# Gated state-space convolution and dense layer: the transforms' second stage and its inverse on sums and differences of mirrored samples

## The chip, the cores and the metric

The kernel runs on one core of one Trainium2 chip. The metric is device time in microseconds for one execution, from launch to the last write. Engines are named as in the profile: PE is TensorE's matmuls, PEld its weight loads, DVE is VectorE, ACT ScalarE, POOL GpSimd and SP SyncE, which here only issues transfers (SPq).

## What is computed

```python
def _A_ref(u, A_re, A_im, B_re, B_im, C_re, C_im, log_dt, Dskip):   # u: 1 x 2048 x 512
    dt = exp(log_dt)[:, None]
    P = exp((dt * A)[:, :, None] * arange(L))                       # 512 x 128 x 2048
    K = einsum("dn,dnl,dn->dl", C, P, dt * B).real                  # the convolution's taps
    y = irfft(rfft(u padded to 2L) * rfft(K padded to 2L))[:L]      # along the 2048 positions
    return y + u * Dskip

def _B_ref(x, w1, b1, w2, b2):                                      # 512 -> 1792 -> 512
    return gelu(x @ w1 + b1) @ w2 + b2

x = A_u
g = sigmoid((x * gate_w).sum(-1, keepdims=True))
return g * _A_ref(x, ...) + (1 - g) * _B_ref(x, ...)
```

All of it is in float32, with 2048 positions and 512 channels.

## The kernel before

The program has two parts. `front` holds the dense layer, the making of the taps, and the first stage of both transforms. `conv` holds the second stages, the product of the spectra, the inverse and the output.

**The transform.** The 2048 positions are split as 64 p + q, with p up to 32 and q up to 64. A first stage transforms over p: its result is, for each of 32 frequencies k0, the real and imaginary parts of 64 values of q, 128 rows by 512 channels. It goes to memory (`tu_d` for the signal, `tk_d` for the taps) and comes back one k0 at a time as a 256 KB tile (`attic` and `loft` for the signal, `tk` for the taps). The second stage multiplies such a tile with a matrix over q, once for the real part and once for the imaginary part of 64 outputs k1.

**`front`** does not run in the order in which it is written. Four generators (`dense`, `taps`, `signal`, `early`) add tasks with an engine, a length and a due time to `Plan`, and `Plan.run` sorts them into one order for each engine. Each engine then runs its instructions strictly in that order. Lengths and due times are constants of the file (`K_0`, `D_S1` and so on). `dense` is the 512-1792-512 layer, in float32 split into a high and a low part, so that each product is three matmuls (L869 to L871 for the first matrix, L917 to L919 for the second). `taps` makes K in 16 contractions of 32 channels (`contract`, L653): 64 matmuls each, of 128 by 32 weights on 64 columns, into the PSUM tile `pk`. ACT copies `pk` to `s1` (L670), and after every second contraction `first_stage` (L378) makes eight matmuls of 32 by 64 weights, two into each of four PSUM banks. ACT copies these into `sk` (L678). After four contractions, eight transfers take `sk` to `tk_d` (L693), in runs of 256 bytes. `signal` loads two tiles of x, runs the same `first_stage` on them, eight times in all, and stores to `tu_d` (L399). POOL's queue carries a memset for each contraction (L605), the loads of `xh` and `xlo` (L772) and the accumulating output transfers (L949).

**`conv`** is written out by hand as 16 steps of two frequencies each. In a step, DVE makes the product of the spectra, six operations on 128x512 (L1106 to L1111, `product`). PE makes the second stage of the next step's signal and of the taps two steps ahead (L1084, `pair`), and this step's inverse (L1123, `inverse`). ACT copies the taps' results out of PSUM (L1092) and the inverse's (L1129, tile `sa`). SP stores each `sa` to `t4_d` (L1131), fetches later tiles of taps and signal (L1059, L1179) and, from step 6 on, the dense layer's output (L1148). Every second step, `matrices` makes on ACT the second half of the weights out of a loaded table `cc` (L1068 to L1071). After every four steps the stored results come back with positions as columns and frequencies as rows in `t3` (L1138), on POOL's queue, the last time on ACT's. After the last step PE does the rest of the dense layer (`rest`, L1159 to L1161) and four matmuls on old data (`warm`, L1197). The last stage (L1208) then multiplies 64 rows of `t3` at a time with 64 by 32 weights. Its results are scaled by the gate and added to the dense output on DVE (L1219), or on ACT and POOL (L1216, L1217), and stored.

## Time and profile before

| what | value |
|---|---|
| time, median of 3 runs | 552.75 us (551.3 to 552.95) |
| span of the profiled execution | 549.7 us |
| PE busy | 528.3 us (96%) |
| DVE busy | 427.2 us (78%) |
| ACT busy | 371.6 us (68%) |
| POOL busy | 41.2 us (7%) |
| transfers | 108.35 MB, 82469 packets, 39446 of them under 512 bytes |
| chain that ended last, by engine | PE 65%, ACT 13%, DMA 7%, issue 6% |

The profile is of one execution. A busy PE says only that a matmul was in its pipeline, since matmuls overlap. The chain that ended last is found by going back from the last instruction to what released it, so it names the work that set the end. A row of instructions gives line, engine, operation, output and inputs, shape, count, busy time and mean nanoseconds of one; a float32 matmul shows as two records, one for each of its passes. In a table of windows each engine has its busy microseconds and its count, then follow the granted clock of PE, the mean busy share of the 16 DMA engines, and the bytes moved per second.

### The profile page before, as it was taken

How to read it: one execution, taken by the hardware profiler on the slowest of the kernel's cores; microseconds unless marked ns; L12 is line 12 of the kernel's file. 1: busy time of each engine (PE TensorE's matmuls, PEld its weight loads, DVE VectorE, ACT ScalarE, POOL GpSimd, SP SyncE). 2: the span in 40 equal slices, each digit the busy share in tenths (PEclk: the TensorE clock that was granted, in tenths of full speed). 3: DMA queues.
4: the chain of work that ended last, by engine and by line, in shares of the span. 5: the costliest groups of instructions: out<-in, count | busy, mean ns of one | idle time of the engine just before them, and what ended most of it. 6: DMA issues, size and time to landing. Idle time of an engine off the chain costs nothing.

```text
span 549.7 us, 12354 instructions
## 1 busy us (share of the span) xinstructions
PE 528.3 (96%) x4882; PEld 394.7 (72%) x4882; DVE 427.2 (78%) x806; ACT 371.6 (68%) x630; POOL 41.2 (7%) x79
## 2 busy tenths in 40 slices
PE   7879999999999999999999999999999999999993
PEld 6547887988798879787988889889889633333450
DVE  6798999999999949879999899999411566666523
ACT  4979847799856599977668987397263654555312
POOL 2000000000000000000101010101011001010104
PEclk9868999999999999999999999999999999999997
DMA  8989573153592442483976136624528979999968
GB/s 252 342 282 312 188 254 113 48 185 111 128 277 97 154 114 80 150 300 63 221 209 183 39 72 149 126 79 109 162 39 184 305 253 302 377 395 377 315 230 305
DMA packets 82469, 108.35 MB, mean 197 GB/s; under 512 B 39446, under 2 KB 42522, under 8 KB 81900
## 3 DMA queue, kind: packets, MB, share of 16 engines
q1 hardware_dynamic: 77020, 86.56, 49.0%
q0 software_dynamic: 5056, 18.65, 13.2%
q10 hardware_dynamic: 336, 2.36, 1.2%
q8 instruction: 38, 0.62, 0.5%
q14 instruction: 19, 0.16, 0.1%
HBM read 61.93 MB, written 45.62 MB: 196 GB/s over the span
## 4 chain that ended last, share of the span: by engine, by line
PE 65%; ACT 13%; DMA 7%; issue 6%; DVE 3%; SPq 2%; POOL 1%; POOLq 0%; ACTq 0%; DVEq 0%
PE pk L653 9%; PE acc L917 7%; PE ph L869 7%; PE ph L871 7%; PE ph L870 7%; PE acc L919 6%; PE acc L918 6%; PE p2u L1084 5%; PE p2k L1084 5%; PE pa L1123 4%; ACT sk L678 2%; PE ph L378 2%; ACT L886 2%; DMA tu_d<-attic 2%; ACT ph L886 1%
## 5 line engine op out<-in xcount | busy, mean ns | idle before, releaser
L869 PE MATMUL ph<-xh,wh 128*128 128x256 f32 x448 | 129.7, 289 | 3.7 <-ACT attic L396 1.5
L871 PE MATMUL ph<-xh,wl 128*128 128x256 f32 x448 | 128.6, 287 | 0.5 <-DVE wl L752 0.4
L870 PE MATMUL ph<-xlo,wh 128*128 128x256 f32 x448 | 128.3, 286 | 0.0
L869 PEld LDWEIGHTS ph<-xh,wh 128*128 128x128 f32 x448 | 86.9, 194 | 13.3 <-issue 4.8
L917 PE MATMUL acc<-wh,hh 128*128 128x512 f32 x210 | 87.1, 415 | 2.6 <-ACT hh L889 2.5
L870 PEld LDWEIGHTS ph<-xlo,wh 128*128 128x128 f32 x448 | 87.0, 194 | 2.0
L871 PEld LDWEIGHTS ph<-xh,wl 128*128 128x128 f32 x448 | 86.9, 194 | 1.1 <-DVE wl L752 1.1
L919 PE MATMUL acc<-wh,hl 128*128 128x512 f32 x210 | 83.0, 395 | 0.0
L918 PE MATMUL acc<-wl,hh 128*128 128x512 f32 x210 | 82.9, 395 | 0.0
L886 ACT ACTIVATE ph<-ph,b1t 128x256 f32<-128x256 f32 x112 | 50.4, 450 | 40.3 <-PE ph L871 38.4
L899 DVE TENSOR_TENSOR hl<-ph,hh 128x512 fp32r<-128x512 f32 (+1 forms) x62 | 38.4, 620 | 37.7 <-ACT hh L889 37.6
L653 PE MATMUL pk<-y,xc 128*32 128x64 f32 x2048 | 61.4, 290 | 0.0
L653 PEld LDWEIGHTS pk<-y,xc 128*32 128x32 f32 x2048 | 57.2, 136 | 3.7 <-issue 1.4
L917 PEld LDWEIGHTS acc<-wh,hh 128*128 128x128 f32 x210 | 39.7, 189 | 21.9 <-issue 11.2
L919 PEld LDWEIGHTS acc<-wh,hl 128*128 128x128 f32 x210 | 39.7, 189 | 10.5 <-DVE hl L899 1.7
L615 DVE TENSOR_TENSOR y<-y,ea 128x64 f32<-128x64 f32 (+4 forms) x80 | 45.4, 567 | 0.2
L918 PEld LDWEIGHTS acc<-wl,hh 128*128 128x128 f32 x210 | 39.8, 189 | 6.0
L889 ACT CAST hh<-ph 128x512 fp32r<-128x512 f32 (+1 forms) x62 | 33.0, 532 | 9.1 <-PE acc L918 7.3
L460 DVE TENSOR_TENSOR loft<-xc,zz 128x256 f32<-128x256 f32 (+2 forms) x48 | 37.3, 777 | 1.7 <-ACT xc L586 1.2
L461 DVE TENSOR_TENSOR loft<-xc,zz 128x256 f32<-128x256 f32 (+2 forms) x48 | 37.2, 775 | 0.0
L628 DVE TENSOR_TENSOR y<-y,loft 128x2048 f32<-128x2048 f32 x16 | 36.6, 2286 | 0.0
L1092 ACT COPY k<-p2k 128x512 f32<-128x512 f32 x32 | 18.7, 586 | 22.0 <-issue 12.2
(172 smaller groups left out, 926.6 us busy)
## 6 DMA issues: line engine op xcount, KB each, us to landing
tu_d<-attic SPq DMA_DIRECT2D x64, 128.0 KB, 3.1
tk_d<-sk SPq DMA_DIRECT2D x32, 256.0 KB, 4.5
tk<-tk_d SPq DMA_DIRECT2D x32, 256.0 KB, 5.6
t_d<-sa SPq DMA_DIRECT2D x32, 256.0 KB, 5.1
t<-t_d POOLq DMA_DIRECT2D x12, 512.0 KB, 6.6
attic<-tu_d SPq DMA_DIRECT2D x22, 256.0 KB, 4.5
attic<-in_xt_dram SPq DMA_DIRECT2D x16, 256.0 KB, 3.9
xh_d<-xh SPq DMA_DIRECT2D x8, 512.0 KB, 3.8
```

Of the source, the lines that this page charges most:

```text
L460: vec(2 * m, lambda: vv.tensor_mul(t, a, br), due, [ka, *kb], [kt])
L615: nc.vector.tensor_mul(both(n, 64 - 3 * n, n), both(0, 64 - n, n), an)
L653: nc.tensor.matmul(pks[q][32 * j : 32 * j + 32, gg], x[:, r, :, ch], y[:, r, :, ch], start=(r == 0), stop=(r == 1), skip_group_check=True,)
L869: nc.tensor.matmul(p, h, xh[xk][:, d], start=(d == 0), stop=False)
L870: nc.tensor.matmul(p, h, xlo[xk][:, d], start=False, stop=False)
L871: nc.tensor.matmul(p, lo, xh[xk][:, d], start=False, stop=(d == 3))
L886: nc.scalar.activation(phs[q][:, n], phs[q][:, n], AF.Gelu_apprx_tanh, bias=b1t[:, f : f + 1])
L899: nc.vector.tensor_sub(lo, phs[q][:, 0:nf], hi.bitcast(F32))
L917: nc.tensor.matmul(a, h, wh[1][w], start=start, stop=False)
L918: nc.tensor.matmul(a, h, wl[1][w], start=False, stop=False)
L919: nc.tensor.matmul(a, l, wh[1][w], start=False, stop=(j == 3))
L1084: nc.tensor.matmul(out[64 * i : 64 * i + 64], w, x, start=True, stop=True)
```

## The change

The tiles that the second stage reads hold sums and differences of mirrored positions in place of real and imaginary parts. The real part of the spectrum then depends on the first 64 rows alone, through cosines, and the imaginary part on the last 64 rows alone, through sines. So each 128 by 64 product becomes a 64 by 64 one, and the same holds for the inverse: 64 by 64 weights into one half of the output's rows, without a second accumulating matmul. The table of weights has four pieces of 384 KB in place of eight of 256 KB, and `matrices` is gone. The recombination of sums and differences moves into the last stage, whose weights grow from 64 by 32 to 128 by 64.

The sums and differences are made on POOL: for the signal from pairs of loaded tiles, 128x512 each, and for the taps from `s1`, 128x256 each, between the contraction and the first stage. For the latter the contraction writes its 64 columns 32 bytes apart in PSUM (`[P, 64, 8]`). The row order of input and output and the order of the channels change with it; the constants that set the planner's due times do not. The diff, without the numbering of rows on the host, the renamed tables of constants and moved declarations:

```diff
+    c1 = np.stack([np.stack([er, ei], 2), np.stack([ei, -er], 2)], 1).reshape(32, 128)
+    c1 = np.tile(c1, (4, 1))
...
+    f2 = np.zeros((32, 2, 2, 32, 64))
+    g2 = np.zeros((32, 64, 32, 2))
     for n, k in enumerate(ko):
-        er, ei = om(4 * (q[:, None] * k + 32 * np.outer(q, k1)) + q[:, None])
-        f2[n, 0], f2[n, 1] = er, -ei
-        er, ei = om(4 * (qn[None] * k + 32 * np.outer(k1, qn)) + qn[None])
-        g2[n, :, :, 0], g2[n, :, :, 1] = er, -ei
-    f2 = f2.reshape(8, 4, P, 64).transpose(0, 2, 1, 3).reshape(8, P, 256)
-    g2 = g2.reshape(8, 2, P, P).transpose(0, 2, 1, 3).reshape(8, P, 256)
+        a = 2.0 * np.pi * (k + 32 * k1 + 0.25) / L
+        f2[n, :, 0] = np.cos(np.outer(m + 0.5, a))
+        f2[n, :, 1] = np.sin(np.outer(m + 0.5, a))
+        g2[n, :, :, 0] = np.cos(np.outer(a, m))
+        g2[n, :, :, 1] = np.sin(np.outer(a, m))
+        g2[n, :, 0, 1] = 1 - 2 * (k1 % 2)
...
-        pks = tiles(N_PK, [P, 8, 64], "pk", space=psum)
+        pks = tiles(N_PK, [P, 64, 8], "pk", space=psum)
         pus = tiles(N_PU, [P, D], "pu", space=psum)
 
-        sk = pool.tile([P, 64, 2, 4, 8], F32, name="sk")
+        sk = pool.tile([P, 32, 4, 4, 8], F32, name="sk")
-        s1 = tiles(2, [P, D], "s1")
+        s1 = tiles(2, [P, 2, 256], "s1")
+        sd = tiles(2, [P, 2, 256], "sd")
...
-                        nc.tensor.matmul(bank[64 * m : 64 * m + 64], c1t[rs], x[rs], start=True, stop=True)
-
-            mm(1.2, products, due + D_S1, [*(key for _, key in xs), "c1"], [key for _, key in banks], 0.5)
+                        nc.tensor.matmul(bank[64 * m : 64 * m + 64], c1t[rs, m], x[rs], start=True, stop=True)
+
+            keys = [k for _, key in xs for k in (key if isinstance(key, list) else [key])]
...
-        rows = tu_d.rearrange("k (c t) d -> (k c) t d", c=2)
+        rows = tu_d.rearrange("k (c e t) d -> (k c) e t d", c=2, e=2)
...
-                xs = [(ux[m], ("ux", m)) for m in range(2)]
                 for m in range(2):
-                    move(256, lambda m=m, s=s: nc.sync.dma_start(ux[m], xl[2 * s + m]), t - 10, [], [("ux", m)])
+                    move(256, lambda m=m, s=s: nc.sync.dma_start(ux[m], xl[s + 8 * m]), t - 10, [], [("ux", m)])
+                k = take("ld", N_LD)
+                pl.add(
+                    "POOL", 1.27, lambda k=k: nc.gpsimd.tensor_add(ld[k], ux[0], ux[1]), t - 9,
+                    [("ux", 0), ("ux", 1)], [("ld", k)],
+                )
+                pl.add("POOL", 1.27, lambda: nc.gpsimd.tensor_sub(ux[1], ux[0], ux[1]), t - 9, [("ux", 0)], [("ux", 1)])
...
-                first_stage(xs, t, evac)
+                first_stage([(ld[k], ("ld", k)), (ux[1], ("ux", 1))], t, evac)
...
-                                pks[q][32 * j : 32 * j + 32, gg],
+                                pks[q][32 * j : 32 * j + 32, :, gg],
...
-            xs, key = s1[c % 2], ("s1", c % 2)
-            act(512, lambda: nc.scalar.copy(xs, pks[q].rearrange("p g s -> p (g s)")), t + D_S1, [("pk", q)], [key])
-            pair.append((xs, key))
-            if c % 2 == 0:
+            e = c % 2
+            xs, key = s1[e], ("s1", e)
+            act(512, lambda: nc.scalar.copy(xs, pks[q].rearrange("p (e s) g -> p e (s g)", e=2)), t + D_S1, [("pk", q)], [key])
+            pl.add(
+                "POOL", 0.7, lambda: nc.gpsimd.tensor_add(sd[0][:, e], xs[:, 0], xs[:, 1]), t + D_S1,
+                [key], [("sd", 0, e)],
+            )
+            pl.add(
+                "POOL", 0.7, lambda: nc.gpsimd.tensor_sub(sd[1][:, e], xs[:, 0], xs[:, 1]), t + D_S1,
+                [key], [("sd", 1, e)],
+            )
+            if e == 0:
...
-                        sk[:, :, c // 2, r].rearrange("p s g -> p g s"),
-                        pp.rearrange("p (g s) -> p g s", g=8),
+                        sk[:, :, cs, r].rearrange("p s e g -> p e s g"),
+                        pp.rearrange("p (e s g) -> p e s g", e=2, g=8),
...
-            first_stage([pair.pop(0), pair.pop(0)], t, evac)
+            first_stage(
+                [(sd[i].rearrange("p a b -> p (a b)"), [("sd", i, 0), ("sd", i, 1)]) for i in range(2)], t, evac
+            )
...
-                n, ss = h % 2, slice(h // 2 * 16, h // 2 * 16 + 16)
-                d = u * UW + n * 64
+                n, ss = h % 2, slice(h // 2 * 8, h // 2 * 8 + 8)
+                d = u * UW
...
-                        tk_d[:, :, d : d + 64].rearrange("k (c s) g -> (k c) s g", c=2)[:, ss],
+                        tk_d[:, :, d : d + UW].rearrange("k (c e s) g -> (k c) e s g", c=2, e=2)[:, n, ss],
...
-            if n % 4 == 0:
-                m = n // 4
-                cc = pool.tile([P, 2, 256], F32, tag="cc", name=f"cc{m}", bufs=4)
-                nc.sync.dma_start(cc, c2[m].rearrange("p (a b) -> p a b", a=2))
-                c4s[m] = cc
+            if n % 8 == 0:
+                m = n // 8
+                cc = pool.tile([P, 768], F32, tag="cc", name=f"cc{m}", bufs=4)
+                nc.sync.dma_start(cc, c2[m])
+                mats[m] = cc[:, 0:512].rearrange("p (n k) -> p n k", n=8), cc[:, 512:768].rearrange("p (n k) -> p n k", n=4)
...
-        def matrices(m):
-
-            cc = c4s[m]
-            f = cc[:, 0].rearrange("p (n k) -> p n k", n=4)
-            f1 = pool.tile([P, 4, 64], F32, tag="f1", name=f"f1{m}", bufs=2)
-            g = cc[:, 1].rearrange("p (s q c) -> p s q c", s=2, c=2)
-            g1 = pool.tile([P, 2, 64, 2], F32, tag="g1", name=f"g1{m}", bufs=2)
-            nc.scalar.mul(f1[0:64], f[64:128], -1.0)
-            nc.scalar.copy(f1[64:128], f[0:64])
-            nc.scalar.mul(g1[:, :, :, 0], g[:, :, :, 1], -1.0)
-            nc.scalar.copy(g1[:, :, :, 1], g[:, :, :, 0])
-            mats[m] = (f, f1), [z.rearrange("p s q c -> p s (q c)") for z in (g, g1)]
...
-        def pair(s, r, c, out):
+        def pair(s, r, outs):
 
             for i in range(2):
                 n = 2 * s + i
-                w = mats[n // 4][0][c][:, n % 4]
                 x = t2s[n] if r else us[n % N_US]
-                nc.tensor.matmul(out[64 * i : 64 * i + 64], w, x, start=True, stop=True)
+                w = mats[n // 8][0][:, n % 8]
+                for c in range(2):
+                    h = slice(64 * c, 64 * c + 64)
+                    nc.tensor.matmul(outs[c][64 * i : 64 * i + 64], w[h], x[h], start=True, stop=True)
...
+            pks = [ps.tile([P, D], F32, tag="pk", name=f"p2k{s}{c}", bufs=2) for c in range(2)]
+            pair(s, 1, pks)
...
-                pas[2 * s + i] = ps.tile([P, D], F32, tag="pa", name=f"pa{s}{i}", bufs=2)
-            for c in range(2):
-                w = mats[s // 2][1][c][:, s % 2]
-                for i in range(2):
-                    r = slice(64 * i, 64 * i + 64)
-                    nc.tensor.matmul(pas[2 * s + i], w[r], v[c][r], start=(c == 0), stop=(c == 1))
+                n = 2 * s + i
+                pas[n] = ps.tile([P, D], F32, tag="pa", name=f"pa{s}{i}", bufs=2)
+                r = slice(64 * i, 64 * i + 64)
+                w = mats[n // 8][1][r, s % 4]
+                for c in range(2):
+                    nc.tensor.matmul(pas[n][64 * c : 64 * c + 64], w, v[c][r], start=True, stop=True)
...
-                nc.sync.dma_start(t4_d[g, :, :, k].rearrange("i c q d -> q (i c) d"), sa)
-                if k < GROUP - 1:
-                    continue
-                rows = t4_d[g].rearrange("i c k q d -> (i c k) q d")
-
-                for h in range(0, 32, 8):
-                    on = nc.gpsimd if n < 31 else nc.scalar
...
+                for c in range(2):
+                    nc.sync.dma_start(t4_d[g, c, :, k].rearrange("e q d -> q e d"), sa[64 * c : 64 * c + 64])
+            if k < GROUP - 1:
+                return
+            rows = t4_d[g].rearrange("c e k q d -> (c e k) q d")
+
+            for h in range(0, 32, 8):
+                on = nc.gpsimd if s < 15 else nc.scalar
...
-            for b in range(4):
-                for i in range(2):
-                    r = slice(64 * i, 64 * i + 64)
+            for i in range(2):
+                for b in range(2):
+                    j = 4 * m + 2 * i + b
                     nc.tensor.matmul(
-                        pbs[i][32 * b : 32 * b + 32], g1t[r], t3[r, 4 * m + b], start=True, stop=True
+                        pbs[i][64 * b : 64 * b + 64], g1t[:, min(j, 1)], t3[:, j], start=True, stop=True```

What follows are rows of the engines' instruction lists, in the order in which each engine runs them: line, operation, output and inputs (the number behind a name is that of the buffer), size of the output. `x2` is two alike, one behind the other.

The first place is PE in `conv`, a second stage of the taps (`p2k`) and the inverse of one step (`pa`). Before:

```order
L1084 MATMUL p2k30_4906<-tk6_4795,cc1_4789 64x512
L1084 MATMUL p2k30_4906<-tk7_4797,cc1_4789 64x512
L1084 MATMUL p2k31_4911<-tk6_4795,f11_4858 64x512
L1084 MATMUL p2k31_4911<-tk7_4797,f11_4858 64x512
L1123 MATMUL pa10_4916<-v10_4892,cc0_4777 128x512
L1123 MATMUL pa11_4917<-v10_4892,cc0_4777 128x512
L1123 MATMUL pa10_4916<-v11_4893,g10_4801 128x512
L1123 MATMUL pa11_4917<-v11_4893,g10_4801 128x512
```

And now:

```order
L1104 MATMUL p2k30_4942<-tk6_4843,cc0_4827 64x512
L1104 MATMUL p2k31_4943<-tk6_4843,cc0_4827 64x512
L1104 MATMUL p2k30_4942<-tk7_4845,cc0_4827 64x512
L1104 MATMUL p2k31_4943<-tk7_4845,cc0_4827 64x512
L1140 MATMUL pa10_4952<-v10_4928,cc0_4827 64x512
L1140 MATMUL pa10_4952<-v11_4929,cc0_4827 64x512
L1140 MATMUL pa11_4955<-v10_4928,cc0_4827 64x512
L1140 MATMUL pa11_4955<-v11_4929,cc0_4827 64x512
```

The number of matmuls is the same; the four of a group now use the four quarters of the array, and all weights come straight from the loaded table.

The second place is POOL in `front`, past the middle of the contractions: the memset of a contraction (`y`), the loads of `xh` and `xlo`, and output transfers from `io`. Before:

```order
L605 MEMSET y_93 128x32
L772 DMA xh10_108<-xh_d_66 128x1024
L772 DMA xlo10_110<-xl_d_67 128x1024
L949 DMA out_0_dram<-io0_143 128x512
L949 DMA out_0_dram<-io1_144 128x512
```

And now:

```order
L629 MEMSET y_93 128x32
L695 TENSOR_TENSOR sd0_107<-s11_106 128x256
L982 DMA out_0_dram<-io0_145 128x512
L699 TENSOR_TENSOR sd1_108<-s11_106 128x256
L982 DMA out_0_dram<-io1_146 128x512
L629 MEMSET y_93 128x32
L805 DMA xh00_109<-xh_d_66 128x1024
L805 DMA xlo00_111<-xl_d_67 128x1024
```

The sum and the difference, which the first stage waits for, have come in between transfers that wait for ACT.

The third place is SP in `conv`, the transfers of one step. Before:

```order
L1131 DMA t4_d_61<-sa2_4771 32x4x512
L1131 DMA t4_d_61<-sa3_4772 32x4x512
L1059 DMA tk14_4926<-tk_d_63 128x512
L1059 DMA tk15_4928<-tk_d_63 128x512
L1179 DMA attic_76<-tu_d_62 128x512 x2
```

And now:

```order
L1150 DMA t4_d_61<-sa2_4821 32x2x512 x2
L1150 DMA t4_d_61<-sa3_4822 32x2x512 x2
L1092 DMA tk14_4964<-tk_d_63 128x512
L1092 DMA tk15_4966<-tk_d_63 128x512
L1197 DMA attic_76<-tu_d_62 128x512 x2
```

Each store of 256 KB has become two of 128 KB; what is fetched is the same.

95 lines of the change are left out of this document (52 added, 43 removed).

## The prediction

> **What bounds the kernel now.** I read the page's slices first (busy tenths of 40 equal parts, 13.7 us each), then a table of windows, then the chain that ended last.
>
> ```profile
> PE   7879999999999999999999999999999999999993
> PEclk9868999999999999999999999999999999999997
> DMA  8989573153592442483976136624528979999968
> ...
> 30.00:200.00 170.00, 167.07 (x1662) 136.57 (x1663) 159.52 (x317) 131.90 (x207) 1.83 (x8) 0.96 0.54 173
> 200.00:410.00 210.00, 209.44 (x2402) 181.17 (x2402) 175.00 (x325) 156.58 (x256) 20.46 (x37) 1.00 0.52 135
> 424.00:532.00 108.00, 106.64 (x479) 44.29 (x478) 62.28 (x101) 50.33 (x104) 6.45 (x13) 1.00 0.93 325
> 440.00:466.00 26.00, 26.00 (x115) 8.45 (x116) 17.26 (x29) 13.32 (x27) 1.12 (x3) 1.00 0.82 272
> 466.00:498.00 32.00, 32.00 (x142) 10.13 (x140) 21.32 (x35) 17.29 (x36) 3.02 (x6) 1.00 1.04 383
> ```
>
> PE is busy from end to end. In `front` DVE is close behind: 159.5 of 170 us, then 175 of 210. In `conv` (424 to 532) DVE and ACT fall to about half, but the transfers rise: a share of 0.93 of the 16 DMA engines, and 1.04, that is full, from 466 to 498, at 383 GB/s. PE and the transfers are both near their limit there. Which one sets the end, the chain says:
>
> ```profile
> 408.07 3.82 ACT sk L678 x4
> 420.20 4.42 DMA tk_d<-sk
> 424.67 5.96 DMA tk<-tk_d
> 430.77 2.09 PE p2k L1084 x7
> ...
> 456.66 1.92 PE pa L1123 x8
> 458.58 1.87 PE p2u L1084 x8
> 460.44 1.72 PE p2k L1084 x8
> ```
>
> In `conv` it is PE: a step is 1.92 + 1.87 + 1.72 = 5.5 us of matmuls without a gap, 16 steps are 88 us. The handover from `front` (408 to 431) goes through ACT and the transfers.
>
> **The 64 by 64 products.** What they cost hangs on whether matmuls in different parts of the array run side by side. Two groups of rows show it:
>
> ```profile
> 406.95 0.65 PE L378 MATMUL ph<-s,c1t 32*64 32x512 f32 x2
> 406.98 0.66 PE L378 MATMUL pu<-s,c1t 32*64 32x512 f32 x4
> 407.43 0.59 PE L378 MATMUL ph<-s,c1t 32*64 32x512 f32 x2
> ...
> 458.99 0.59 PE L1084 MATMUL p2u<-attic,cc 128*64 128x512 f32 x1
> 458.99 0.59 PE L1084 MATMUL p2u<-loft,cc 128*64 128x512 f32 x1
> 459.42 0.59 PE L1084 MATMUL p2u<-attic,f 128*64 128x512 f32 x1
> ```
>
> In the first stage all eight tiles, four groups of rows by two of columns, start within 0.03 us, and their second passes 0.48 us later. In `conv` today two tiles start together, and the next pair 0.43 us on. So a pass costs 0.43 us however many tiles share it. Four matmuls of two passes are today four pairs, 1.72 us; as four quarters of the array they are two, 0.86 us. Each row half writes its own bank, as in the first stage. A step's three groups then take 2.6 us in place of 5.5, and PE is no longer the bound.
>
> **What bounds `conv` next.** DVE and ACT first:
>
> ```profile
> 459.70 0.69 DVE L1106 TENSOR_TENSOR v<-p2u,k 128x512 f32<-128x512 f32 x1 [1.81 <-ACT sa L1129]
> 460.31 0.68 DVE L1107 TENSOR_TENSOR v<-p2u,k 128x512 f32<-128x512 f32 x1
> ...
> L1092 ACT COPY k<-p2k 128x512 f32<-128x512 f32 x32 | 18.7, 586 | 22.0 <-issue 12.2 <-PE p2k L1084 7.2 <-ACT g L1071 2.7
> L1129 ACT COPY sa<-pa 128x512 f32<-128x512 f32 x32 | 17.2, 589 | 23.3 <-PE pa L1123 17.4 <-issue 5.9
> ...
> 459.22 1.18 SPq L1131 DMA_DIRECT2D t_d<-sa  x2
> ```
>
> DVE starts an operation every 0.61 us: six make 3.7 us a step, 58 us in all. ACT has four copies, 2.4 us (the weights made on ACT fall away; they lay beside PE). The transfers take longer. From 424 to 532 they carry 108 us x 325 GB/s = 35.1 MB. Of these the smaller table of weights saves seven loads of 256 KB for three of 384 KB, some 0.65 MB; nothing else that `conv` moves is less. 34.5 MB at 383 GB/s are 90 us, that is 5.6 us a step: just what PE takes today. What is gained is that the engines never wait for PE, as they do in the window from 440 to 466 at 272 GB/s. Begun at 424.7 as now, they end at 514.7. One pause stays, between the last `sa` and the last load of `t3`:
>
> ```profile
> 521.64 1.08 ACT L1129 COPY sa<-pa 128x512 f32<-128x512 f32 x2 [3.11 <-issue]
> 525.78 2.44 ACTq L1138 DMA_DIRECT2D t<-t_d  x4
> ...
> 532.77 3.93 PE L1208 MATMUL pb<-t,g1t 64*32 64x512 f32 x64
> 537.79 3.67 PE L1208 MATMUL pb<-t,g1t 64*32 64x512 f32 x64 [1.09 <-DVE attic L1219]
> 543.97 0.84 SPq L1221 DMA_DIRECT2D out_dram<-attic  x1
> ```
>
> It is 525.8 - 522.7, 3 us. So the last stage can start near 518.5 instead of 532.8: **14 us earlier**. If the transfers keep only the 325 GB/s of the whole window, 34.5 MB take 106 us and the gain is nothing. If prefetching hid all of them and DVE were the bound, its 58 us from 432 (the handover, then taps, signal and two copies), then 2 us for inverse and copy, 3 for the pause and 6 for the last load would end at 501, 31 us earlier. I take the full rate, since the fetches run four steps ahead, and 6 to 20 as its own range. SP issues four stores of 128 KB a step in place of two; two now hold it 1.18 us of 5.5, so even twice that fits.
>
> **The last stage.** It goes from eight tiles side by side (64 rows by 32 columns) to two (128 by 64), with half the matmuls: 32, as 16 pairs of two passes, 16 x 2 x 0.43 = 13.8 us, where 3.93 + 3.67 = 7.6 now do. Today its end is set by the stores: the last is issued at 544.0, some 2.5 us after the last matmul, and ends with the span at 549.7. Spread over 13.8 us, 4.2 MB ask for 305 GB/s, so stores no longer queue, and PE sets the end:
>
> ```profile
> L1219 DVE SCALAR_TENSOR_TENSOR attic<-pb,gate,attic 128x512 f32<-128x512 f32 x6 | 4.4, 748 | 1.6 <-PE pb L1208 1.3
> out_dram<-attic ACTq DMA_DIRECT2D x1, 256.0 KB, 3.6
> ```
>
> 13.8 + 0.2 to drain + 0.75 + about 0.4 of issue + 3.6 = 18.8 us against 549.7 - 532.8 = 16.9: **2 us later**. Bounds: nothing, if the stores would have lasted as long anyway, and 5 us if the clock is halved for a window or two.
>
> **The handover.** The copies into `sk` now write runs of eight, and the stores to `tk_d` runs of 512 bytes in place of 256:
>
> ```profile
> L678 ACT COPY sk<-pu 128x512 f32<-128x512 f32 x16 | 17.0, 1171 | 0.0
> L670 ACT COPY s<-pk 128x512 f32<-128x512 f32 x16 | 9.4, 585 | 5.3 <-DVE pk L667 5.1
> L1084 PE MATMUL p2k<-tk,cc 128*64 128x512 f32 x64 | 18.3, 593 | 1.4 <-DMA tk<-tk_d 1.4
> ```
>
> A copy costs between 0.59 us (contiguous) and 1.17 (scattered). Either way, and with half as many runs to write between 412 and 424.7, the `tk` tiles come sooner than now, while PE still has the dense layer to do. I take PE's wait of **1.4 us** as gone, and no more, since the matmuls before it stay.
>
> **`front`.** PE has the same matmuls. POOL gets 16 operations on 128x512 and 32 on 128x256:
>
> ```profile
> L1217 POOL TENSOR_TENSOR attic<-attic,sa 128x512 f32<-128x512 f32 x4 | 5.0, 1269 | 1.1 <-ACT sa L1216 1.1
> L949 POOL DMA_DIRECT2D out_dram<-io x14 | 12.3, 1009 | 57.7 <-ACT io L938 57.7
> L653 PE MATMUL pk<-y,xc 128*32 128x64 f32 x2048 | 61.4, 290 | 0.0
> 67.69 3.77 PE pk L653 x127
> ```
>
> At 1.27 and, by size, some 0.65 us these are 20 + 21 = 41 us, on an engine with 22 us of work in 380. Each of the eight first stages of the taps comes 1.3 us later after its contraction, and PE, which runs in order, has mostly 12 or more matmuls of the dense layer in between, which cover it. Behind an output transfer that waits for ACT (POOL waited 57.7 us for those, with nothing urgent behind it) a difference can be late. The tasks also fall into another order. I charge **3 us**, between 0 and 8. The clock adds **1 us**: PE will be busy half the time in `conv`, and in the third slice, 27 to 41 us, where PE was busy 0.7, the granted clock fell to 0.6. Half speed makes a step 5.2 us, still under the 5.6 of the transfers, so it costs only at the edges.
>
> The sum, on the profiled 549.7: -14 + 2 - 1.4 + 3 + 1 = 540.3. The median of the runs lies 3.0 us above the span, so **543 us**, and 534 to 551 as this case's own range.
>
> **Rivals.** *POOL against DVE, slower.* POOL now reads SBUF for 41 us while DVE works. DVE's idle time in the two windows of `front` is 10.5 + 35 us. By 200 us some 24 of the 41 have run (six of the eight sums for the signal, 15 us, and seven contractions, 9). If each costs DVE as much, `front` grows by 24 - 10.5 = 14 us at least, and by 41 at most if DVE's idle time, in which it waits for ACT and PE, can take up none. I take 20: 543 + 20 - 3 = 560. It decides from about 13 us, a third of the 41. For it speaks that nearly every DVE operation in `front` reads two tiles of SBUF; against it that L1219 takes 748 ns while POOL adds in the last stage, though its one operand is in PSUM. So the trace cannot tell. The Trainium skill (SBUF — State Buffer, Who interferes with whom) says that a DVE instruction with two SBUF inputs contends with a GpSimd instruction that reads SBUF; by that rule this rival would hold in some measure, and no run here shows it.
>
> *Scattered writes to PSUM, slower.* The contraction's matmuls write 32 bytes apart. They take 3.77 us for 128 records, so four side by side take 0.118 us for 64 columns, 1.84 ns a column; a pass of 512 columns in 0.43 us takes 0.84. So writes could be 2.2 times as slow and stay hidden. If they lengthen the contractions by half, 16 x 3.77 / 2 = 30 us come on top: 573. It decides from a quarter. The Trainium skill (PSUM — Partial Sum Buffer, Specifications) says that any non-contiguous pattern slows matmuls significantly; by that rule the time would be on this side, and no matmul here writes that way.
>
> *The transfers give nothing.* If they keep the average rate of the whole window, PE's saved time turns into waits for `tk` and `t3`: 543 + 14 = 557, or 552 if `front` costs nothing.
>
> **How the numbers follow.** The forecast has 0.55, POOL against DVE 0.20 (a quarter of it mild enough to end faster), scattered writes 0.10, the transfers 0.10, and 0.05 is left for an order of `front` that stalls PE by more than 10 us, near 555. Changes under 0.3% (1.7 us) can't be told from none. Faster, same and slower: of the forecast 0.51, 0.03, 0.01; of POOL against DVE 0.04, 0.02, 0.14; of the transfers 0, 0.02, 0.08; the other two all slower, 0.15. Together 0.55, 0.07 and 0.38. The range runs from 533 up to 569, so that it takes in the mild half of the rivals and leaves the worst of the scattered writes out.
>
> **What would show it.** Right: in `conv` `p2k`, `p2u` and `pa` start four at a time and a group takes 0.86 us; the DMA share stays at 1.0 from 432 to about 510; the last stage starts near 518 and PE works 13.8 us in it. Wrong: DVE groups of L460 or L628 with longer means than 688 and 2286 ns (the first rival), contractions over 3.8 us (the second), a last stage that starts after 528 with a share below 0.95 (the third). A first stage of the taps that waits for POOL for more than 1 us each time would break the charge for `front`.

## The result, and the profile after

The change makes the kernel **slower**: 584.4 us median of 4 runs (582.3 to 588.2) against 552.1 us for the kernel before on the same chip, a ratio of 1.058 with a 95% interval of [1.053, 1.062]. Predicted were 543 us, with a range of 533 to 569. The profiled execution took 588.2 us, of which 586.2 are its span.

First the windows, cut where the parts meet: `front` from 30 us to the first matmul of `conv` (`p2k`), `conv` to the first matmul of the last stage (`pb`), and the last stage. A row has the stretch and its length, the busy time and count of PE, PEld, DVE, ACT and POOL, then PE's granted clock, the share of the transfer engines, and GB/s. The kernel before:

```profile
30.00:430.80 400.80, 395.95 (x4193) 335.61 (x4194) 338.14 (x648) 299.40 (x483) 24.00 (x47) 0.98 0.55 154
430.80:532.80 102.00, 102.00 (x439) 39.05 (x440) 60.47 (x98) 46.19 (x95) 6.18 (x12) 1.00 0.92 329
532.80:549.70 16.90, 7.57 (x129) 2.29 (x128) 7.23 (x10) 4.12 (x6) 7.51 (x6) 0.82 0.68 254
```

And the changed kernel:

```profile
30.00:458.60 428.60, 399.96 (x4192) 336.73 (x4192) 364.87 (x648) 287.50 (x482) 79.75 (x93) 0.96 0.51 146
458.60:562.90 104.30, 70.85 (x438) 33.64 (x436) 60.47 (x100) 35.28 (x67) 6.20 (x12) 0.88 0.92 306
562.90:586.20 23.30, 16.57 (x64) 5.19 (x64) 7.51 (x10) 4.12 (x6) 7.64 (x6) 0.87 0.59 225
```

All three parts are longer: `front` by 28 us, `conv` by 2 where 14 were to be gained, the last stage by 6. In `front` PE does the same matmuls (4193 and 4192 records), but now stands idle for 28.6 us where it stood idle for 4.9, and DVE is busy 26.7 us longer with the same 648 instructions. In `conv` PE falls from 102 busy microseconds to 71, and nothing comes of it: the transfers move 32 MB (104.3 x 306) at 306 GB/s where they moved 33.6 at 329.

The slices of the page, and the chain that ended last, say the same:

```profile
PE   7958799994989999999999989999999995557855
DVE  6897989998999984985999998999911699364023
PEclk9659889998999999999999998999999999787969
...
PE 33%; DVE 31%; DMA 18%; ACT 8%; issue 5%; SPq 3%; POOL 0%; ACTq 0%; DVEq 0%; POOLq 0%
```

Before, the chain was PE for 65% and DVE for 3%. Now DVE has 31% and the transfers 18%. So there are two questions: what made DVE and the waits of PE in `front` longer, and why do the transfers not fill the time that PE gave up.

### The profile page after: what moved, and what is told of

It is laid out like the page before. It is cut to its first block, busy times and chain, and to the rows that moved or that the text cites. A ratio compares the mean times of both kernels' runs of the same rounds, so it can differ in the third digit from the quotient of the medians.

```text
span 586.2 us, 12283 instructions
## 1 busy us (share of the span) xinstructions
PE 513.0 (88%) x4818; PEld 395.3 (67%) x4818; DVE 455.4 (78%) x806; ACT 349.4 (60%) x600; POOL 99.7 (17%) x127
## 2 busy tenths in 40 slices
PE   7958799994989999999999989999999995557855
DVE  6897989998999984985999998999911699364023
## 3 DMA queue, kind: packets, MB, share of 16 engines
q10 hardware_dynamic: 336, 2.36, 1.1%
## 4 chain that ended last, share of the span: by engine, by line
PE 33%; DVE 31%; DMA 18%; ACT 8%; issue 5%; SPq 3%; POOL 0%; ACTq 0%; DVEq 0%; POOLq 0%
DMA tk<-tk_d 7%; PE pk L675 5%; DVE y L639 5%; PE acc L950 4%; DVE loft L484 3%; PE acc L952 3%; DVE loft L485 3%; PE acc L951 3%; DVE phase L584 3%; PE pb L1224 3%; PE ph L902 3%; PE ph L904 3%; PE ph L903 3%; PE p2k L1104 2%; PE ph L396 2%
## 5 line engine op out<-in xcount | busy, mean ns | idle before, releaser
L950 PE MATMUL acc<-wh,hh 128*128 128x512 f32 x210 | 88.2, 420 | 3.7 <-ACT hh L922 3.7
L952 PE MATMUL acc<-wh,hl 128*128 128x512 f32 x210 | 84.8, 404 | 7.5 <-DVE hl L932 7.5
L951 PE MATMUL acc<-wl,hh 128*128 128x512 f32 x210 | 84.2, 401 | 0.0
L675 PE MATMUL pk<-y,xc 128*32 128x64 f32 x2048 | 62.2, 291 | 8.7 <-ACT s L693 7.5
L675 PEld LDWEIGHTS pk<-y,xc 128*32 128x32 f32 x2048 | 57.2, 138 | 13.7 <-ACT s L693 8.2
L932 DVE TENSOR_TENSOR hl<-ph,hh 128x512 fp32r<-128x512 f32 (+1 forms) x62 | 38.1, 614 | 25.4 <-ACT hh L922 25.1
L950 PEld LDWEIGHTS acc<-wh,hh 128*128 128x128 f32 x210 | 40.2, 192 | 23.4 <-issue 12.0
L639 DVE TENSOR_TENSOR y<-y,ea 128x64 f32<-128x64 f32 (+4 forms) x80 | 55.0, 687 | 0.9
L952 PEld LDWEIGHTS acc<-wh,hl 128*128 128x128 f32 x210 | 40.4, 192 | 19.7 <-DVE hl L932 10.7
L1104 PE MATMUL p2k<-tk,cc 64*64 64x512 f32 x128 | 26.7, 688 | 22.4 <-DMA tk<-tk_d 21.8
L922 ACT CAST hh<-ph 128x512 fp32r<-128x512 f32 (+1 forms) x62 | 33.0, 532 | 15.4 <-PE acc L951 12.7
L484 DVE TENSOR_TENSOR loft<-xc,zz 128x256 f32<-128x256 f32 (+2 forms) x48 | 38.2, 796 | 0.5
L485 DVE TENSOR_TENSOR loft<-xc,zz 128x256 f32<-128x256 f32 (+2 forms) x48 | 37.5, 782 | 0.0
L652 DVE TENSOR_TENSOR y<-y,loft 128x2048 f32<-128x2048 f32 x16 | 36.5, 2282 | 0.1
```

The lines of the kernel that those rows point to most:

```text
L484: vec(2 * m, lambda: vv.tensor_mul(t, a, br), due, [ka, *kb], [kt])
L485: vec(2 * m, lambda: vv.tensor_mul(v, a, bi), due, [ka, *kb], [kv])
L639: nc.vector.tensor_mul(both(n, 64 - 3 * n, n), both(0, 64 - n, n), an)
L675: nc.tensor.matmul(pks[q][32 * j : 32 * j + 32, :, gg], x[:, r, :, ch], y[:, r, :, ch], start=(r == 0), stop=(r == 1), skip_group_check=True,)
L950: nc.tensor.matmul(a, h, wh[1][w], start=start, stop=False)
L951: nc.tensor.matmul(a, h, wl[1][w], start=False, stop=False)
```

## Experiments: POOL's sums

The first suspicion is the first rival: POOL reads SBUF beside DVE. In the changed kernel a group of DVE operations with two SBUF inputs, and the sums on POOL themselves, stand so (line, operation, count, busy time, mean ns of one):

```profile
L639 DVE TENSOR_TENSOR y<-y,ea 128x64 f32<-128x64 f32 (+4 forms) x80 | 55.0, 687 | 0.9
```

```profile
L695 POOL TENSOR_TENSOR sd<-s 128x256 f32<-128x256 f32 x16 | 15.7, 981 | 62.0 <-ACT s L693 62.0
L413 POOL TENSOR_TENSOR attic<-attic,ux 128x512 f32<-128x512 f32 x8 | 15.7, 1958 | 47.2 <-DMA ux<-in_xl_dram 19.0 <-DVE xc L487 10.0 <-DVE wl L785 6.4
```

The same DVE group took 567 ns before:

```profile
L615 DVE TENSOR_TENSOR y<-y,ea 128x64 f32<-128x64 f32 (+4 forms) x80 | 45.4, 567 | 0.2
```

But the kernel has more changes in `front`: the first stage waits for the sums, the order of all tasks is new, and some instructions have new forms, which come further down. Three runs take the sums and the waits for them apart. In all three the first stage takes unsummed tiles, so that PE does not wait for POOL, and the planner sees the same tasks as in the changed kernel.

**Sums that nobody reads.** POOL adds as before, into tiles that are not used:

```diff
-                pl.add("POOL", 1.27, lambda: nc.gpsimd.tensor_sub(ux[1], ux[0], ux[1]), ...)
-                first_stage([(ld[k], ("ld", k)), (ux[1], ("ux", 1))], t, evac)
+                pl.add("POOL", 1.27, lambda k=k: nc.gpsimd.tensor_sub(ld[k], ux[0], ux[1]), ...)
+                first_stage([(ux[1], ("ld", k)), (ux[1], ("ux", 1))], t, evac)
...
-                [(sd[i].rearrange("p a b -> p (a b)"), ...) for i in range(2)], t, evac
+                [(s1[i].rearrange("p a b -> p (a b)"), ...) for i in range(2)], t, evac
```

> The changed kernel, in which GpSimd still makes every sum and difference of real tiles at the same place, but nobody reads them: the first stage takes the unsummed tiles (of the signal one tile twice), so the result is left wrong and PE never waits for GpSimd. If GpSimd's operations slow DVE (in the trace the DVE operations beside them are 26.5 us over their form's median), front stays long: the first p2k near 455 to 459 us as now (458.6), DVE busy 450 to 456, total 578 to 585. If the waiting for sums is what costs, p2k comes at 431 to 438, total 555 to 564.

Measured: 584.1 us, ratio 1.056 [1.051, 1.061], the first `p2k` at 460.1, and DVE busy 363.9 us in `front` as in the changed kernel. The time of the changed kernel is there without any wait of PE for a sum.

**No sums.** The four operations become empty tasks (`None` in place of the instruction).

> As the one before, with the 48 GpSimd operations left out altogether and every other task in the same order. Contention: p2k at 431 to 438 us, DVE busy 427 to 430, total 556 to 564 (what is left over 552 is conv and the last stage). If the changed order of the tasks is to blame, it stays near 584.

Measured: 572.9 us, ratio 1.035 [1.028, 1.043]. Neither expectation: 11 us are gone, and 19 over the kernel before remain. Its window:

```profile
30.00:449.60 419.60, 396.55 (x4196) 336.95 (x4196) 339.57 (x646) 287.40 (x482) 24.02 (x47) 0.96 0.52 149
```

DVE is back at its old busy time, 339.6, but PE still stands idle for 23 us. So POOL's work costs 11 us in this order of tasks, and something else in `front` costs more.

**Constants in place of sums.** POOL writes as many elements to the same places and reads none (`nc.gpsimd.memset(..., 0.0)`).

> As the first, but GpSimd writes constants of the same size to the same places instead of adding: no reads of SBUF. If it is GpSimd's reads of SBUF that slow DVE, as the run without sums (p2k 431 to 440, total 556 to 566). If any work of GpSimd at SBUF slows DVE, DVE's operations beside it grow too and the total lies over 570.

Measured: 571.7 us, ratio 1.032 [1.028, 1.037], like the run without sums. The window of `front`, and the group of DVE operations from above:

```profile
30.00:443.70 413.70, 394.31 (x4196) 334.52 (x4196) 340.60 (x648) 287.75 (x482) 37.47 (x89) 0.97 0.53 152
L639 DVE TENSOR_TENSOR y<-y,ea 128x64 f32<-128x64 f32 (+4 forms) x80 | 45.2, 565 | 0.9
```

POOL is busy 13 us longer than without sums, and DVE 1 us; with the unread sums it was 55 us of POOL (79.5 against 24.0) and 24 of DVE. Constants take POOL less time than sums, but even per microsecond of POOL's work DVE loses only a sixth as much. So it is operations of POOL that read which slow DVE, and not its writes. The Trainium skill (SBUF — State Buffer, Who interferes with whom) says just this, that a DVE instruction with two SBUF inputs contends with a POOL instruction that reads SBUF and not with one that only writes it; the two runs agree with it on both counts. Two groups for which the trace names a single tile as input grew as well, by 2.0 us (L584, 28.8 to 30.8) and 1.1 us (L641, 2.8 to 3.9); which of them this rule covers was not looked into.

## Experiments: the order of the tasks

What is left in `front` could be the new order or the new forms (scattered writes of the contraction, other copies and stores). Two runs give the changed kernel the old order. The planner is told only of the tasks of the kernel before, and the sums are issued inside the load or the copy that they follow:

```diff
+        def fetch(m, s):
+            nc.sync.dma_start(ux[m], xl[s + 8 * m])
+            if m == 1:
+                nc.gpsimd.tensor_add(us_, ux[0], ux[1])
+                nc.gpsimd.tensor_sub(ux[1], ux[0], ux[1])
...
+            def split():
+                nc.scalar.copy(xs, pks[q].rearrange("p (e s) g -> p e (s g)", e=2))
+                nc.gpsimd.tensor_add(sd[:, e], xs[:, 0], xs[:, 1])
+                nc.gpsimd.tensor_sub(xs[:, 1], xs[:, 0], xs[:, 1])
+            act(512, split, t + D_S1, [("pk", q)], [key])
```

**Old order, with sums.**

> The changed kernel with all its arithmetic, but the order of tasks that the kernel before has: the planner does not see GpSimd's sums, which are issued right behind the load or the copy that they need. With order and contention as two separate losses (15 and 12 us by the runs so far): the first p2k at 440 to 447 us, DVE busy 448 to 456, total 566 to 573. If the order was the only loss, as the next run. If the order of before cannot take the sums at all (PE waits for GpSimd): 580 or more.

**Old order, without sums** (the lines on `gpsimd` left out).

> As the one before without the sums (result left wrong): the contraction with scattered writes, the copies and stores of the changed kernel, in the order of tasks of the kernel before. If the order alone made the run without sums 573 instead of 558, this one is 555 to 561 with the first p2k at 430 to 434 us. If the new forms of the instructions cost it, it stays at 568 to 576.

Measured: 572.3 us (1.034 [1.028, 1.040]) with sums, as expected, and 553.1 us (0.998 [0.994, 1.002]) without, below both of its ranges. The window of the run without sums:

```profile
30.00:423.40 393.40, 389.61 (x4195) 333.20 (x4194) 335.75 (x644) 284.27 (x479) 24.03 (x47) 0.99 0.54 157
```

And of the one with them:

```profile
30.00:447.30 417.30, 401.92 (x4200) 339.21 (x4198) 360.45 (x650) 287.01 (x482) 87.38 (x93) 0.97 0.53 150
```

Without sums the order is worth 572.9 - 553.1 = 20 us, and PE's idle time goes from 23 to 4 us. In the old order the sums cost 19 us rather than 11. DVE loses the same 25 us in both; that PE hides less of them where it has no other waits is likely, but was not tried. The stops also come with a lower granted clock: with sums, the same matmuls keep PE busy 12 us longer (401.9 against 389.6), at a mean clock of 0.97 in place of 0.99, which by itself is some 8 us (an estimate from these two figures). Of PE's waits in the run with sums, these two name POOL:

```profile
PE ph L397 <- POOL us__107 L410: 3.7, 1, 3.7
...
PE ph L397 <- POOL ux L411: 1.1, 1, 1.1
```

Which part of the change upset the order? Four more runs without sums, in which the planner sees one cause at a time.

> No sums are made in this run and the next three (result left wrong, first stages take unsummed tiles), so only the order of tasks differs. Here the planner sees the sums of the taps as empty tasks and those of the signal not at all. If the taps' tasks make the order that costs 15 to 20 us (573 against 553 and 558), 566 to 574 and PE idle 15 us or more between 30 us and the first p2k; if the signal's do, 550 to 557 and 4 to 7 us idle.

> The planner sees the signal's sums (with their place in the ring of loads) as empty tasks, and not those of the taps. If the signal's tasks make the dear order, 566 to 574 and PE idle 15 us or more; if not, 550 to 557.

> As the one before, but the signal's sum takes no place in the ring of six loads, which the weights and inputs of the dense layer share. If it is the place in the ring that makes the order dear (loads of weights come later), 550 to 558 and PE idle 4 to 9 us; if the tasks' own time and waits in the plan do, 566 to 574.

> The reverse of the one before: a place in the ring of loads is skipped for each step of the signal, and the planner sees no task for the sums. The place in the ring: 566 to 574. The tasks: 550 to 558. If any disturbed order is dear, whatever disturbed it, this one and the one before both lie at 560 or more.

| what the planner sees | median us | ratio to before | PE idle, 30 us to `p2k` |
|---|---|---|---|
| tasks of the taps | 551.8 | 0.996 [0.993, 1.000] | 5 |
| tasks of the signal, with a place in the ring | 566.6 | 1.023 [1.016, 1.031] | 16 |
| tasks of the signal, no place | 561.8 | 1.014 [1.008, 1.020] | 12 |
| the place alone | 563.7 | 1.018 [1.012, 1.024] | 17 |

Taken alone, the sums of the taps, the ones with a short deadline, disturb nothing (551.8 against 553.1 us). It is the signal's, and either half of them alone, the tasks or the place among the loads, costs 9 or 11 us, both together 13.5. From there to the 572.9 us of the new order without sums 6 us are left, which no run explains. The planner's constants are values with many digits that were set for one set of tasks; here one further set left the order as good as it was, and three others gave orders in which PE waits. What PE waits for in such an order, in the changed kernel from 25 to 430 us (engine, line, releaser, total, times, longest):

```profile
PE acc L952 <- DVE hl L932: 7.5, 5, 3.5
PE pk L675 <- ACT s L693: 7.5, 1, 7.5
PE ph L396 <- POOL attic L413: 5.5, 1, 5.5
PE acc L950 <- ACT hh L922: 3.3, 3, 2.3
```

No single wait carries it: the dense layer's own matmuls (`acc`) wait more often than anything new, and only 5.5 us name POOL. Without sums, the wait of 5.5 us stands at the same place with the load of `ux` as its releaser. How the order makes these waits stays open.

## Experiments: conv

**conv alone.** The kernel before, with `conv` and its tables from the changed kernel. `front` makes no sums there, so its tiles are not the ones that `conv` means.

> The kernel before with conv alone taken from the changed kernel (64 by 64 products, halved stores, last stage of 128 rows, their tables); front is that of before, so no sums are made and the result is left wrong. The prediction's own terms: -14 for conv, +2 for the last stage: 538 to 542. What the trace of the changed kernel shows (conv 104.3 instead of 102.0, last stage 23.3 instead of 16.9): no gain, 555 to 563, with a mean rate of transfers near 310 GB/s in conv.

Measured: 558.1 us, ratio 1.012 [1.005, 1.019]. Its `conv`:

```profile
431.80:530.80 99.00, 73.59 (x436) 34.82 (x437) 59.37 (x98) 34.38 (x64) 6.19 (x12) 0.89 0.94 322
```

99 us where 87.7 were predicted, with the transfer engines at 0.94: not idle, but slow, at 322 GB/s. The longest waits of SP's stores in the same run, from 425 to 532 us, are for older stores, and then for ACT's copies:

```profile
SPq L1130 <- DMA t_d<-sa: 9.7, 6, 2.6
SPq L1130 <- ACT sa L1127: 5.1, 6, 2.8
```

SP's 364 transfers use eight semaphores in turn, and none of the 223 for which the landing of the one eight before is in the trace is issued ahead of that landing. So, as far as the trace shows, at most eight are under way. A step of `conv` had six or seven transfers on SP and now has two more, so the eight hold fewer bytes. The waits alone prove nothing, as the next run shows, where SP waits for older transfers no less (28 us in the same stretch, against 22 here).

**Whole stores.** One store of 256 KB for a result in place of two of 128 KB. The weights of the inverse get their columns in another order, `t4_d` and the last weights their rows, so that the store is contiguous in memory too:

```diff
-                for c in range(2):
-                    nc.sync.dma_start(t4_d[g, c, :, k].rearrange("e q d -> q e d"), sa[64 * c : 64 * c + 64])
+                nc.sync.dma_start(t4_d[g, k].rearrange("c e q d -> (c e q) d"), sa)
```

> The kernel with conv alone changed (no sums, result left wrong), and each result of conv stored as one transfer of 256 KB in place of two of 128 KB. If small stores keep too few bytes on their way, conv (first p2k to first pb, 99 us with halves) falls to 92 to 96 us at 345 GB/s or more, and the total to 548 to 554. If the transfer engines are simply full (their share there is already 0.92 to 0.99), it stays at 556 to 561.

Measured, with conv alone: 544.9 us, ratio 0.986 [0.981, 0.990], better than expected:

```profile
431.70:518.80 87.10, 71.82 (x434) 32.89 (x435) 59.29 (x98) 34.19 (x64) 6.18 (x12) 0.92 0.99 369
```

The last stage starts at 518.8, and 518.5 was predicted. The same edit on the changed kernel:

> The changed kernel with one edit: each result of conv is stored as one transfer of 256 KB (the weights of the inverse put the columns in another order, the last table its rows, so the result stays the same). front is untouched, so the first p2k stays at 456 to 461. If halving the stores costs what the runs with conv alone showed (558.1 against 544.9), the total is 568 to 573 and conv takes 86 to 92 us in place of 104. If that gain belongs to the other front only, 580 or more.

Measured: 569.9 us, ratio 1.028 [1.022, 1.035], `conv` 87.1 us from 462.2. The stores cost 12 to 14.5 us: 13.2 between the medians with conv alone and 11.6 between the profiled spans, 14.5 and 14.4 on the changed kernel.

**Why halves are dear.** A half differs from a whole store in its size, in the partitions that it covers, and in that it is not contiguous in memory. Three runs on conv alone:

> conv alone changed (558.1, result left wrong), the stores still halved, but every second half issued by GpSimd in place of SP. If what halves cost is the number of transfers that SP may have on its way (each waits for the eighth before it), SP carries as many as with whole stores and the total falls to 544 to 550. If each transfer of 128 KB is dear in itself, it stays at 555 to 561.

> conv alone changed (no sums, result left wrong). A step stores its two results as two transfers of 256 KB, but each takes 64 partitions (one half of both results) in place of 128. If the loss of the halved stores is their number and size (few bytes on their way), conv is as with whole stores: 87 to 89 us from the first p2k to the first pb, 360 GB/s or more, total 544 to 550. If it is that a transfer covers only 64 of 128 partitions, conv stays at 97 to 100 us and 322 GB/s, total 555 to 561.

> conv alone changed (result left wrong). The reverse of the one before: four transfers of 128 KB a step, each over all 128 partitions and half of the columns (1 KB in a piece in place of 2). Number and size: 97 to 101 us in conv at 315 to 325 GB/s, total 555 to 562. Partitions: 87 to 90 us, 355 GB/s or more, total 544 to 551.

Their edits, against whole stores the last two:

```diff
-                    nc.sync.dma_start(t4_d[g, c, :, k]...
+                    (nc.sync, nc.gpsimd)[c].dma_start(t4_d[g, c, :, k]...
...
+            for c in range(2):
+                rows = t4_d[g, k - 1 : k + 1, c].rearrange("i e q d -> (e q) i d")
+                nc.sync.dma_start(rows, sas[s % 3][64 * c : 64 * c + 64])
...
+                for c in range(0, D, 256):
+                    nc.sync.dma_start(t4_d[g, k]...[:, c : c + 256], sa[:, c : c + 256])
```

| store | partitions | `conv`, us | GB/s | median us, ratio |
|---|---|---|---|---|
| 256 KB | 128 | 87.1 | 369 | 544.9, 0.986 [0.981, 0.990] |
| 256 KB, halves of two results | 64 | 91.1 | 352 | 551.7, 0.996 [0.992, 1.000] |
| 128 KB, halves of the columns | 128 | 94.1 | 342 | 555.2, 0.998 [0.993, 1.003] |
| 128 KB, halves of the rows | 64 | 99.0 | 322 | 558.1, 1.012 [1.005, 1.019] |
| the same, every second one by POOL | 64 | 91.3 | 350 | 553.0, 0.998 [0.994, 1.002] |

(`conv` and its rate are from one profile each; the medians of the five stand in the same order. The last two rows keep the layout in memory of the changed kernel.) Neither pure expectation came true; both theories hold a part. From the first row, half the partitions cost 4 us by the profiles and 7 by the medians, half the size 7 and 10, both 12 and 13. So each costs something by itself, and whether they add up is not shown: by the profiles they nearly do, by the medians they do not. All runs here with whole stores of 128 partitions take 87 to 89 us in `conv`, and those with halves of the rows on SP alone 98 to 104, so a difference of 3 us between two single profiles says little. Moving half of the small stores off SP's queue gives back 8 us in the profile and 5 in the medians. (The third row also has pieces of 1 KB in place of 2, which may be a part of what the size costs; the last row, whose pieces have 2 KB, does not share that doubt. In the second row a store waits for both copies of its step, which may be a part of what the partitions cost.) That few bytes are on their way thus has two runs behind it, which went about it differently; that 64 partitions cost by themselves has one. The Trainium skill (SBUF — State Buffer, Door 1: The DMA port swizzle) says that partitions 0 to 63 reach only half of SBUF's 16 ports and partitions 0 to 127 all of them; the runs agree in sign.

## Experiments: the best of both

**Old order and whole stores**, with all sums on POOL:

> All the arithmetic of the changed kernel, the order of tasks of the kernel before, and whole stores. The differences of the runs added up: 566 to 573 less what whole stores give (0 to 6): 560 to 573. Order the only loss and whole stores a gain: 548 to 556.

Measured: 556.3 us, ratio 1.007 [1.004, 1.010], between the two ranges: whole stores gave 16 us here (572.3 - 556.3). `conv` takes 87.0 us, so what remains lies in `front`, where POOL's sums cost the 19 us from above, and in the last stage.

**Sums on PE.** PE adds in any case. For the signal, the two mirrored tiles are loaded as halves of one tile's 64 rows, with the weights stacked below each other, once with a minus; for the taps, two matmuls add up in PSUM:

```diff
+                    rs = slice(64 * (r % 2), 64 * (r % 2) + 64)
+                        nc.tensor.matmul(bank[64 * m : 64 * m + 64], c1t[rs, m], ux[r // 2][rs], start=True, stop=True)
...
+            for h in range(2):
+                for r, (bank, _) in enumerate(banks):
+                    for m in range(2):
+                        nc.tensor.matmul(bank[64 * m : 64 * m + 64]..., c1t[rs, m * (1 + (r + h) % 2)], s1[rs, :, h], start=(h == 0), stop=(h == 1), ...)
```

> All the arithmetic, order of tasks of the kernel before, whole stores, and the sums and differences made by PE: for the signal 64 rows at a time with the weights stacked, for the taps two matmuls that add up in PSUM. GpSimd makes none. If GpSimd's reads are what is left of the loss (556.3 here, 544.9 without sums in conv alone), DVE busy falls to 425 to 429 and PE pays 0.5 to 1 us for each of 16 first stages: the first p2k at 432 to 441, total 546 to 553. If something else of the sums holds front, 555 or more.

Measured: 548.8 us, ratio **0.988 [0.983, 0.994]**: with all of the arithmetic, 1.2% faster than the kernel before, clear of the noise. Its `front`:

```profile
30.00:439.30 409.30, 402.29 (x4326) 338.34 (x4324) 336.38 (x644) 286.27 (x482) 24.00 (x47) 0.99 0.53 153
```

DVE is back at 336 us. PE's 16 first stages keep it busy 32 us (16.4 for the signal, 15.8 for the taps) where they took 21 with the old order and no sums and 24 in the kernel before, and it is idle for 7.

**A warmer last stage.** `N_KEEP = 8` in place of 4.

> The run with sums on PE, in which PE's idle matmuls ahead of the last stage are eight in place of four (3.5 us more), so that PE does not stop while the last tiles of t3 come. There the first half of the last stage ran at a granted clock of 0.73 (525 to 530), and from the first pb to the end of the span it took 22.6 us where 18.8 were predicted and 16.9 were taken before. If the clock is what is over, the last stage falls to 20 to 21 us and the total to 546 to 548. If not, the last stage stays at 22 to 23 us and the total at 548 to 550.

Measured: 547.6 us, ratio 0.990 [0.987, 0.994], not to be told from the run before. In its trace PE does not stop:

```profile
526.93 0.64 PE L1226 MATMUL pb<-t,g1t 128*64 128x512 f32 x1
...
527.41 7.40 PE L1226 MATMUL pb<-t,g1t 128*64 128x512 f32 x31
535.67 7.09 PE L1226 MATMUL pb<-t,g1t 128*64 128x512 f32 x32 [0.86 <-DVE attic L1237]
```

From the first `pb` to the end it is 548.6 - 526.9 = 21.7 us, against 22.6. The clock was worth 1 us, less than had been hoped for, and `conv` took 1.7 us more in this profile.

## Why the prediction was wrong, point by point

*The 64 by 64 products: right.* PE's rows in `conv` after, one step (start, duration, operation, count, and the idle time before it):

```profile
468.27 1.17 PE L1140 MATMUL pa<-v,cc 64*64 64x512 f32 x5 [0.28 <-DVE v L1127]
469.15 0.59 PE L1104 MATMUL p2u<-attic,cc 64*64 64x512 f32 x1
...
470.01 0.59 PE L1104 MATMUL p2k<-tk,cc 64*64 64x512 f32 x1
...
471.86 0.61 PE L1140 MATMUL pa<-v,cc 64*64 64x512 f32 x1 [0.28 <-DVE v L1127]
```

`p2u` starts 0.88 us after `pa`, and `p2k` 0.86 us after `p2u`. This step, which waits for no transfer, takes 3.6 us, at whose end PE waits for DVE, as worked out (3.7 us). The mean step takes 6.5 (104.3 / 16).

*What bounds `conv` next: the right bound, and the first step that failed.* "Two now hold it 1.18 of 5.5 us, so even twice that fits" counted the time in which SP issues, and not how many bytes transfers of half the size keep on their way, nor that they cover half the partitions. The rate fell to 306 GB/s where 383 were taken. With whole stores the step's number holds: 87.1 us against 87.7, 369 GB/s. So the 14 us were there, and the halved stores took them. (The terms of the prediction give 514.7 + 3 = 517.7 for the start of the last stage; 0.8 us of its 518.5 stand under no term.) The rival "the transfers give nothing" had the outcome, 0.10, but another cause: it expected PE's time to turn into waits at the average rate, while the rate itself fell.

*The rest of `front`: the charge of 3 us, the second step that failed, and the larger one.* It failed for two reasons. The order of tasks, which the charge took in without a price of its own, costs 20 us (0.05 had been put on one of more than 10). And POOL's reads slow DVE, the first rival (0.20). Its size was near: 26.7 us more of DVE's busy time, of which 11 reached the end in this order and 19 in the old one, where 20 were named. The test that had been set for it looked in the wrong place. L460 and L628, now L484 and L652, hardly moved (in the kernel before, the group of 48 at L460 had a mean of 777 ns, and L628 2286):

```profile
L484 DVE TENSOR_TENSOR loft<-xc,zz 128x256 f32<-128x256 f32 (+2 forms) x48 | 38.2, 796 | 0.5
...
L652 DVE TENSOR_TENSOR y<-y,loft 128x2048 f32<-128x2048 f32 x16 | 36.5, 2282 | 0.1
```

The loss sat in other groups, such as L639, and there in its small forms: 128x64 went from 220 to 356 ns and 128x1024 from 1220 to 1215. The waits of PE for POOL, for which the 3 us mainly stood, cost nothing in the new order: the run with unread sums takes as long. Put together, by the medians, order (20), sums (11), the new forms (5 less) and the rest of the change with conv alone (4.5) make 30.5 of the 32 us that the kernel lost.

*Scattered writes to PSUM: no cost seen.*

```profile
101.64 3.77 PE pk L675 x127
```

A contraction takes 3.77 us as before. The Trainium skill (PSUM — Partial Sum Buffer, Specifications), which expects any non-contiguous pattern to slow matmuls significantly, is not borne out by these matmuls of 64 columns that write 32 bytes apart, four side by side. Writes up to 2.2 times as slow would have stayed hidden, by the prediction's own estimate, so that they cost nothing by themselves is not shown.

*The handover: right, and more.*

```profile
437.40 2.06 ACT sk L709 x4
```

The four last copies take 2.06 us in place of 3.82. From the start of the last contraction to the first `p2k` it is 37.8 us with the new forms in the old order, against 39.2 before: 1.4, as predicted, and PE no longer waits for `tk` there. Over all, these forms in the old order brought conv alone from 558.1 to 553.1 us; where the rest of these 5 us comes from was not looked into.

*The last stage: mechanism right, size off.* PE stops for 8.3 us ahead of it, for `t3`, and then takes 9.5 + 7.1 us:

```profile
562.88 9.50 PE L1224 MATMUL pb<-t,g1t 128*64 128x512 f32 x32 [8.26 <-DMA t<-t_d]
573.23 7.09 PE L1224 MATMUL pb<-t,g1t 128*64 128x512 f32 x32 [0.84 <-DVE attic L1235]
```

Predicted were 13.8 us. The second half nearly keeps to that; the first takes 2.4 us more, after the stop, at a lower granted clock (the third figure from the end):

```profile
560.00:565.00 5.00, 2.12 (x6) 0.85 (x8) 0.10 (x1) 0.00 (x0) 0.00 (x0) 0.50 0.87 328
565.00:570.00 5.00, 5.00 (x18) 1.56 (x16) 1.55 (x3) 1.37 (x2) 1.45 (x2) 0.72 0.21 79
570.00:575.00 5.00, 4.16 (x21) 1.24 (x18) 2.10 (x3) 1.33 (x2) 2.36 (x2) 1.00 0.80 302
```

Between its two halves PE waits 0.84 us, for DVE to free a PSUM tile, and from its end to the end of the span it is 5.9 us where 5 were taken. Together 23.3 against 18.8, and 6.4 later than before, beyond the 5 that had been named as the bound. Where PE had stopped for 2.5 us only, the clock cost about 1 us, as the run with more idle matmuls showed.

The sum, on the profiled execution: 586.2 us against 540.3 predicted are 46 too many. `conv` has 16.6 of them (104.3 less 87.7), the last stage 4.5, and the first `p2k` at 458.6 in place of 432.4 has 26; that these are about one too many is the 1 us that was charged for the clock by itself.

## What to carry to other kernels

A change that frees the bounding engine hands the bound to the next resource, so what the change does to that one, here the size and span of each transfer, has to be priced with the same care as what it saves. Where an order was tuned for one set of tasks, a new order can cost more than the added tasks themselves, as it did here for tasks with plenty of slack and not for those with little: try the old order first, with the new work slipped in where its inputs are made. Work given to an idle engine is not free where it reads the memory of a busy one; here the engine that was busiest did it more cheaply, by adding in the matmul.

## What was not expected of the hardware

Two halves of a store cost more than the whole in two ways, in a stretch of 87 us that moves 32 MB: 128 KB in place of 256 KB a transfer cost 7 us by the profiles and 10 by the medians, 64 in place of 128 partitions 4 and 7. The transfer engines' busy share hides it, with 0.94 at 322 GB/s and 0.99 at 369. And small stores issued from two queues ran as well as stores twice as large from one (91.3 and 91.1 us, medians 553.0 and 551.7, both of 64 partitions).
